# Batch 1's value copies shared by GpSimd and ScalarE, its q loaded ahead of its v, scores and AV moved ahead of transposes, and five unread matmuls fewer

## The chip, the cores and the metric

The kernel runs on one core of one Trainium2 chip. The metric is the time of one execution on the device, in microseconds (us); lower is better. Times vary by about 1% between runs of one kernel (253.42 to 256.43 us in four runs of the kernel before). Every run comes with the TensorE clock that it was granted on average (1.000 is full speed).

Names: PE is TensorE's matmul stream, DVE is VectorE, ACT is ScalarE, POOL is GpSimd. AV is the product of the attention weights and v. In this kernel PSUM holds the results of the matmuls, in tiles that the source calls banks, and SBUF the other tiles. Tiles in the traces: `tkq` and `tv` are the results of `kq_chunk` and `v_chunk` in PSUM, `kqt` and `vt` their copies in SBUF; `qk` are scores, `e_all` exponentials, `av_ps` the AV, `x_ps` transposes; `g_ps`, `v_ps` and `o_ps` are the FFN's gate, value and output products, `th_sb` a tanh, `gs_sb` and `h` what VectorE makes of them.

## The reference, cut to what matters

The first half is block-sorted attention, the second a gated feed-forward block (FFN). Batch 4, 8 heads, 768 rows, head size 64, 8 blocks of 96 rows.

```python
def _attn_ref(q, k, v, sort_net):
    ...                                   # P: sort_net after 5 Sinkhorn rounds
    k_sorted = np.einsum('bhij,bhjcd->bhicd', P, k_b)   # mix the 8 blocks of k
    v_sorted = np.einsum('bhij,bhjcd->bhicd', P, v_b)   # and of v
    scores = scale * np.matmul(q_b, k_sb.transpose(0, 1, 2, 4, 3))
    ...                                   # softmax over each 96x96 block
    return np.matmul(attn, v_sb)

def _moe_ref(x, w_gate, w_val, w_out):
    g = x @ w_gate                        # (3072, 512) @ (512, 1536)
    silu = g * (1.0 / (1.0 + np.exp(-g)))
    val = x @ w_val
    return silu * val @ w_out
```

## The kernel before

The kernel works in bf16 and handles the 3072 tokens as eight FFN blocks of 384 tokens, `ffn(0)` to `ffn(7)`. While TensorE runs one FFN block, the attention work of later tokens is woven into its stream (`merge`): each side task has a place, counted in estimated TensorE microseconds of the FFN block.

Batch 1 needs three things before its attention can start. Its k and q (`kq`) are mixed and transposed by TensorE (`kq_chunk`). Its v is first re-laid in SBUF from (row, feature) to (feature, row) by plain copies into `vch` (`copy_v`), then mixed by TensorE (`v_chunk`). One `v_chunk` reads all rows of `vch`, so it needs every copy.

```python
def copy_v(eng, pair, rows, s, n=4):              # part s of n of the 96 rows
    cs = slice(s * (C // n), (s + 1) * (C // n))
    dst = vch3[rows, :, cs]
    src = v_tiles[pair][rows, cs, :]
    if eng is nc.scalar:
        eng.copy(dst, src.transpose([0, 2, 1]))
    else:
        eng.tensor_copy(dst, src.transpose([0, 2, 1]))
...
for m in range(0, DF, 256):
    load_gv(m, m + 256)                           # the weights, all on one DMA queue
load_k(1, 0, C)
load_v(1, 0, C)
load_q(1, 0, C)
nc.gpsimd.dma_start(out=wo_sb, in_=wo_dram)       # the output weights, last
...
man = tc.manual_schedule(engines={ET.PE, ET.Pool})
man.__enter__()                                   # from here PE and POOL keep program order;
                                                  # the scheduler orders ACT and DVE
...
load_k_pair()
for s in range(4):
    copy_v(nc.gpsimd, 0, highr, s)                # batch 1's v: all four quarters on GpSimd
...
merge(ffn(0), units(0, range(4, 8), (0.0, 5.6)))
merge(ffn(1), kqs(1, (0.3, 2.6, 4.9)) + vs(v_chunk, 16, (6.2, 7.3, 8.4, 9.5)) + units(1, range(4), (11.0, 15.6)))
for s in range(4):
    copy_v(nc.gpsimd, 1, both, s)
nc.vector.memset(kqt_tile("p")[:, 2 * GI * C:], 0.0)
```

`units(b, ...)` are the scores, exponentials (ACT), AVs and transposes of a batch. `fill(tile, n)` issues n matmuls of zeros that nobody reads; they keep TensorE busy during the start. `gate` and `value` take their PSUM banks from a pool ("gen") of three: a gate bank comes free after a tanh on ACT and a product on DVE.

With `manual_schedule`, the source fixes the order of TensorE and GpSimd only. The order of ScalarE and VectorE is chosen when the kernel is compiled.

The softmax here doesn't subtract the row's maximum and nothing guards it: scores larger than these inputs give would overflow.

Of the kernel before, what the change touches and what calls it, by code (L numbers as in the profile page):

```python
# [17 lines left out]
def kernel(  # L18
# [11 lines left out]
    nc = tc.nc  # L30
# [3 lines left out]
    C = S // NB  # L34
# [6 lines left out]
    NKC = DM // 128  # L41
# [42 lines left out]
    def kq_tile(b):  # L84
        if b not in kq_tiles:
            kq_tiles[b] = natp.tile([128, C, D], BF16, name=f"kq{b}", tag="nat")
        return kq_tiles[b]

    def load_k(b, lo, hi):
        nc.gpsimd.dma_start(out=kq_tile(b)[0:R, lo:hi, :], in_=k_nat[b, :, lo:hi, :])  # L90
# [6 lines left out]
    def load_q(b, lo, hi):  # L97
        nc.gpsimd.dma_start(out=kq_tile(b)[R:2 * R, lo:hi, :], in_=q_nat[b, :, lo:hi, :])

    def load_v(b, lo, hi):  # L100
        if b // 2 not in v_tiles:
            v_tiles[b // 2] = vnp.tile([128, C, D], BF16, name=f"v{b // 2}", tag="vn")
        u = b % 2
        nc.gpsimd.dma_start(out=v_tiles[b // 2][u * R:(u + 1) * R, lo:hi], in_=v_nat[b, :, lo:hi, :])
# [4 lines left out]
    def load_gv(lo, hi):  # L109
        load_w(wg_sb, wg_dram, lo, hi)  # L110
        load_w(wv_sb, wv_dram, lo, hi)

    def copy_v(eng, pair, rows, s, n=4):
# [8 lines that stand above are left out]
    ident = const.tile([128, 128], BF16)  # L122
    lowr, highr = slice(0, R), slice(R, 2 * R)
# [16 lines left out]
    for m in range(0, DF, 256):  # L140
        load_gv(m, m + 256)
    load_k(1, 0, C)
    load_v(1, 0, C)
    load_q(1, 0, C)
    nc.gpsimd.dma_start(out=wo_sb, in_=wo_dram)

    rmix = {b: const.tile([128, 2, 2, H2, NB], BF16, name=f"rmix{b}") for b in (0, 1, "p")}
# [29 lines left out]
    def pair_tile(name, tag):  # L177
        return psum.tile([128, 1024], FP32, name=name, tag=tag)

    def bank_tile(name, tag="gen"):  # L180
        return psum.tile([128, 512], FP32, name=name, tag=tag, bufs=3 if tag == "gen" else 1)
# [29 lines left out]
    def drain(eng, dst, src):  # L211
        if eng == "v":
            nc.vector.tensor_copy(dst, src)  # L213
        else:
            nc.scalar.copy(dst, src)  # L215
# [68 lines left out]
    def exps(b, u, wide, pss):  # L284
        n = ecount[0] % 8
        ecount[0] += 2
        if wide is None:
            for two in range(2):
                nc.scalar.activation(e_all[:, n + two, 0:4 * C], pss[two][0:C, 0:4 * C], AF.Exp, scale=scale)
        else:  # L290
            nc.scalar.activation(e_all[:, n:n + 2, 0:4 * C], wide[0:C, :, 0:4 * C], AF.Exp, scale=scale)  # L291
        es[(b, u)] = [e_all[:, n, :], e_all[:, n + 1, :]]

    def qk(b, u, tag="b"):
        exps(b, u, *scores(b, u, tag))

    def av(b, u, tag="a"):
        half, g = divmod(u, H2)
        vt = vts[b // 2][:, b % 2].rearrange("p (h i) e -> p h i e", h=H)
        av_ps = pair_tile("av_ps", tag).rearrange("p (two n) -> p two n", two=2)  # L300
        o = av_ps[:, :, 0:4 * (D + 1)].rearrange("p two (i e) -> p two i e", e=D + 1)
        for two in range(2):
            e = es[(b, u)][two]
            for i4 in range(4):
                nc.tensor.matmul(o[:, two, i4, :], lhsT=e[:, i4 * C:i4 * C + 128],  # L305
                                 rhs=vt[:, 2 * g + two, half * 4 + i4, :],
                                 start=True, stop=True)
        r_sb = ssp.tile([C, 2, 4, 1], FP32, name="r_sb", tag="r")
        nc.vector.reciprocal(r_sb, o[0:C, :, :, D:D + 1])  # L309
        st = ssp.tile([C, 4, 2, D], BF16, name="st", tag="st")  # L310
        nc.vector.tensor_tensor(st.rearrange("p i two d -> p two i d"), o[0:C, :, :, 0:D],  # L311
                                r_sb.to_broadcast([C, 2, 4, D]), op=ALU.mult)
        sts[(b, u)] = st

    def xt_tile(tag, n):
        bank = psum.tile([128, 1024], BF16, name="x_ps", tag=tag, bufs=3 if tag == "gen" else 1)
        return bank[:, 0:n * 4 * C].rearrange("p (g a b) -> p g a b", g=n, b=C)

    def x_to(dst, b, u):
        st = sts.pop((b, u))  # L320
        for i4 in range(4):
            nc.tensor.transpose(dst[:, i4, :], st[:, i4].rearrange("p a b -> p (a b)"),
                                ident[0:C, 0:C])
# [89 lines left out]
    idle_ps = bank_tile("idle_ps", "x")  # L413

    def fill(tile, n):
        for _ in range(n):
            nc.tensor.matmul(tile, lhsT=warm_sb[:, 0:128], rhs=warm_sb, start=True, stop=True)  # L417
# [37 lines left out]
    fill(idle_ps, 2)  # L455
    v_chunk(0, 0, 8, "v", "gen")
    v_chunk(0, 8, 16, "s", "a")
    fill(idle_ps, 2)
    v_chunk(0, 24, 16, "v", "b")
    fill(idle_ps, 2)  # L460
    v_chunk(0, 40, 8, "s", "gen")
    v_chunk(0, 48, 8, "v", "gen")
    v_chunk(0, 56, 8, "s", "gen")
# [17 lines left out]
    idle_ps = bank_tile("idle_ps")  # L481
# [3 lines left out]
    av(0, 1, "b")  # L485
    fill(idle_ps, 1)
    xts[(0, 0)] = xtp.tile([128, H2, TW], BF16, name="xt0_0", tag="xt")
    x01 = xt_tile("x", 2)
    x_to(x01[:, 0], 0, 0)
    fill(idle_ps, 1)  # L490
    qk(0, 3, "gen")
    av(0, 2, "a")
    x_to(x01[:, 1], 0, 1)
    drain("s", xts[(0, 0)][:, 0:2, :], x01.rearrange("p g a b -> p g (a b)"))
    fill(idle_ps, 2)
# [6 lines left out]
    def early(n, kcs):  # L502
        sb, m, name = ((wg_sb, 0, "g_ps"), (wv_sb, 0, "v_ps"), (wg_sb, 1, "g_ps"))[n]
        if n not in first:
            first[n] = psum.tile([128, TW], FP32, name=name, tag="gen", bufs=3)
        for kc in kcs:
            nc.tensor.matmul(first[n], lhsT=sb[:, kc, ts(m, 128)], rhs=xts[(0, 0)][:, kc, :],
                             start=(kc == 0), stop=(kc == NKC - 1))

    early(0, (0,))  # L510
    early(1, (0,))
    x3 = xt_tile("x", 1)
    x_to(x3[:, 0], 0, 3)
    drain("v", xts[(0, 0)][:, 3:4, :], x3.rearrange("p g a b -> p g (a b)"))
    early(0, (1, 2))
    early(1, (1, 2))
    early(0, (3,))
    early(1, (3,))
    early(2, range(NKC))
    gate_out(0, 0, first[0])  # L520
    value_out(0, 0, first[1])
    gate_out(0, 1, first[2])
# [5 lines left out]
    def units(b, us, ats):  # L528
        us = list(us)
        todo = []  # L530
        for n, at in enumerate(ats):
            u, u2 = us[2 * n:2 * n + 2]
            held = []
            todo.append((at, lambda u=u, u2=u2, held=held: (qk(b, u, "b"), held.append(scores(b, u2, "a")))))
            todo.append((at + 1.3, lambda u2=u2, held=held: exps(b, u2, *held[0])))
            for w, tag, t in ((u, "b", 1.9), (u2, "a", 3.6)):
                if b < 2:
                    todo.append((at + t, lambda w=w, tag=tag: av(b, w, tag)))
                    todo.append((at + t + 3.1, lambda w=w: drain("v", *xtr(b, w))))
                else:  # L540
                    todo.append((at + t, lambda w=w, tag=tag: (av(b, w, tag), x_dma(b, w))))
        return todo

    def kqs(b, ats):
        return [(at, lambda n=n: (kq_chunk(b, n * 32, 16, "v", "b"), kq_chunk(b, n * 32 + 16, 16, "s", "a")))
                for n, at in enumerate(ats)]

    def vs(f, size, ats):
        return [(at, lambda m=m: f(1, m * size, size, "sv"[m % 2], "ba"[m % 2])) for m, at in enumerate(ats)]

    def merge(main, side):
        done, k = 0.0, 0
        side = sorted(side, key=lambda t: t[0])
        for c, f in main:
            f()
            done += c
            while k < len(side) and side[k][0] <= done:
                side[k][1]()
                k += 1
        while k < len(side):  # L560
            side[k][1]()
            k += 1

    def ffn(n):
        todo = []
        for m in range(NFC):
            if n > 0 or m > 1:
                todo.append((0.65, lambda m=m: gate(n, m)))
            if n > 0 or m > 0:
                todo.append((0.65, lambda m=m: value(n, m)))  # L570
            if n > 0 and m % 4 == 3:
                for part in range(3):
                    todo.append((0.87, lambda m=m, part=part: outp(n - 1, m // 4, part)))
        return todo

    load_k_pair()
    for s in range(4):
        copy_v(nc.gpsimd, 0, highr, s)
    load_v(2, 0, C)
    load_v(3, 0, C)  # L580
    q_cast(2)
    q_cast(3)
    both = slice(0, 128)
    merge(ffn(0), units(0, range(4, 8), (0.0, 5.6)))
    merge(ffn(1), kqs(1, (0.3, 2.6, 4.9)) + vs(v_chunk, 16, (6.2, 7.3, 8.4, 9.5)) + units(1, range(4), (11.0, 15.6)))
    for s in range(4):
        copy_v(nc.gpsimd, 1, both, s)
    nc.vector.memset(kqt_tile("p")[:, 2 * GI * C:], 0.0)
# [42 lines left out]
```

## Time and profile before

| | before |
|---|---|
| time, first three runs | 253.42, 253.81, 256.43 us; median 253.81 |
| span of the profiled run | 252.2 us, clock 1.00 |
| TensorE busy | 240.6 us, 95% |

From the profile's page: the line of busy us per engine, with the share of the span and the instruction count, then TensorE's busy tenths and its granted clock in 40 slices of 6.3 us.

```profile
PE 240.6 (95%) x2574; PEld 143.3 (57%) x2574; DVE 159.3 (63%) x342; ACT 110.5 (44%) x187; POOL 51.8 (21%) x46
...
PE   5799999699999999999999999999999999999994
...
PEclk9999999999999999999999999999999999999999
```

TensorE is full from the third slice on, except for one 6 and the last slice. The waits view, with the columns total us, times and longest us, names that dip:

```profile
PE tkq L235 <- DMA kq<-in_q_dram: 2.1, 1, 2.1
```

TensorE waits 2.1 us for q of batch 1, from 46.97 to 49.02 us. The next fence is GpSimd's timeline (start, length, engine, line, operation; in brackets its idle time just before and what ended it). The first three lines are the issues of the loads of v, q and `wo_sb`.

```profile
29.11 0.53 POOL L104 DMA_DIRECT2D v<-in_v_dram  x1 [0.83 <-DMA wv_sb<-in_moe_w_val_dram]
30.70 0.52 POOL L98 DMA_DIRECT2D kq<-in_q_dram  x1 [1.06 <-DMA wg_sb<-in_moe_w_gate_dram]
31.75 1.05 POOL L145 DMA_DIRECT2D wo_sb<-in_moe_w_out_dram  x1 [0.54 <-DMA wv_sb<-in_moe_w_val_dram]
...
44.88 11.22 POOL L120 COPY vch<-v 64x1536 bf16<-64x1536 bf16 x4 [9.90 <-DMA v<-in_v_dram]
```

v has landed when the copies start, at 44.88 us, and q at 48.9. The DMA view gives `wo_sb` 24.2 us from issue to landing, so it lands at 55.95 us.

Two more pieces of before's trace are needed later. The first is ScalarE's timeline around 36 us. ScalarE alternates tanh (`th_sb`) and exponentials (`e_all`) and is idle half of the time (busy 44% of the span).

```profile
35.85 0.49 ACT L364 ACTIVATE th_sb<-g_ps 128x384 bf16<-128x384 f32 x1 [1.17 <-PE g_ps L356]
36.96 1.50 ACT L291 ACTIVATE e_all<-qk 96x768 bf16<-96x768 f32 x2 [0.61 <-PE qk L278]
38.36 0.49 ACT L364 ACTIVATE th_sb<-g_ps 128x384 bf16<-128x384 f32 x1
```

The second is VectorE's timeline from 50 us on.

```profile
49.76 1.23 DVE L213 CAST kqt<-tkq 128x1024 bf16<-128x1024 f32 x1 [1.67 <-PE tkq L235]
50.93 0.07 DVE L588 MEMSET kqtp<- 128x16 uint32 x1
...
64.52 1.22 DVE L213 CAST vt<-tv 96x1024 bf16<-96x1024 f32 x1
```

The second line is the `memset` that ends the code shown above. In the source it stands behind all of `merge(ffn(1), ...)`, and so behind VectorE's cast of a value chunk of batch 1, the third line, which ran at 64.52 us. It ran at 50.93 us. So the compile did move an instruction of an engine without fixed order over 13 us ahead of work on the same engine that stands before it in the source.

### The profile page before, as it was taken

To read this page: it belongs to the slowest core of one execution; us is meant where nothing else is said; L and a number is where in the kernel's file an instruction comes from. 1 tells how busy PE (TensorE), PEld (TensorE's weight loads), DVE (VectorE), ACT (ScalarE), POOL (GpSimd) and SP (SyncE) were. 2 spreads that over 40 slices of the span, in tenths; PEclk is the share of its full clock that TensorE was granted. 3 is DMA by queue.
4 is the path that set the end of the run, shared out by engine and by line. 5 is a ranking of instruction groups with operands and counts; after the bars stand their busy time and mean duration, and the time that the engine had idled before them with its cause. 6 is when DMAs were issued, how large, how long until landed. Compare 5 with 4: busy or idle time off the path is not lost.

```text
span 252.2 us, 6061 instructions
## 1 busy us (share of the span) xinstructions
PE 240.6 (95%) x2574; PEld 143.3 (57%) x2574; DVE 159.3 (63%) x342; ACT 110.5 (44%) x187; POOL 51.8 (21%) x46
## 2 busy tenths in 40 slices
PE   5799999699999999999999999999999999999994
PEld 5275566466555666666656555555555565555543
DVE  6768788675756866758668457545854685456700
ACT  3966644256442543455543433443444243332311
POOL 7847430899079000000000000000000000000000
PEclk9999999999999999999999999999999999999999
DMA  6959999999999176110113122111111111100122
GB/s 104 210 88 163 196 215 219 195 227 216 218 160 146 42 169 128 44 42 3 42 24 83 42 46 54 49 44 33 60 57 42 34 57 57 44 9 32 44 83 84
DMA packets 37866, 23.98 MB, mean 95 GB/s; under 512 B 26064, under 2 KB 34000, under 8 KB 37328
## 3 DMA queue, kind: packets, MB, share of 16 engines
q0 software_dynamic: 21328, 14.16, 38.3%
q1 hardware_dynamic: 16512, 9.45, 13.1%
q8 instruction: 20, 0.33, 0.5%
q14 instruction: 6, 0.05, 0.1%
HBM read 28.32 MB, written 7.86 MB: 143 GB/s over the span
## 4 chain that ended last, share of the span: by engine, by line
PE 74%; DMA 15%; DVE 3%; POOL 3%; issue 2%; ACT 1%; DVEq 0%; POOLq 0%
PE o_ps L391 23%; PE v_ps L374 21%; PE g_ps L356 20%; DMA kq<-in_q_dram 7%; DMA kq<-in_k_dram 4%; DMA wg_sb<-in_moe_w_gate_dram 4%; PE tkq L235 3%; PE av_ps L305 2%; PE qk L278 2%; PE tv L257 1%; DVE gs_sb L366 1%; PE o_ps L407 1%; DVE vt L213 1%; POOL wg_sb L107 1%; POOL wv_sb L107 1%
## 5 line engine op out<-in xcount | busy, mean ns | idle before, releaser
L366 DVE SCALAR_TENSOR_TENSOR gs_sb<-th_sb,g_ps 128x384 bf16<-128x384 bf16 x96 | 52.7, 549 | 52.9 <-ACT th_sb L364 50.7
L374 PE MATMUL v_ps<-xt,wv_sb 128*128 128x384 bf16 x380 | 77.3, 326 | 0.3
L356 PE MATMUL g_ps<-xt,wg_sb 128*128 128x384 bf16 x376 | 76.5, 325 | 0.0
L364 ACT ACTIVATE th_sb<-g_ps 128x384 bf16<-128x384 f32 x96 | 47.2, 491 | 57.7 <-PE g_ps L356 54.9
L391 PE MATMUL o_ps<-wo_sb,h 128*128 128x512 bf16 x276 | 64.5, 379 | 0.0
L379 DVE SCALAR_TENSOR_TENSOR h<-v_ps,gs_sb 128x384 bf16<-128x384 f32 x96 | 53.3, 555 | 6.9 <-DVE gs_sb L366 0.5
L374 PEld LDWEIGHTS <-wv_sb 128*128 128x128 bf16 x380 | 35.4, 97 | 23.6 <-issue 1.5
L356 PEld LDWEIGHTS <-wg_sb 128*128 128x128 bf16 x376 | 34.6, 97 | 22.9
L391 PEld LDWEIGHTS <-h 128*128 128x128 bf16 x276 | 26.1, 98 | 27.7
L396 ACT COPY o_sb<-o_ps 128x512 f32<-128x512 f32 x23 | 13.5, 586 | 51.4 <-PE o_ps L391 51.4
L120 POOL COPY vch<-v 64x1536 bf16<-64x1536 bf16 (+1 forms) x10 | 28.0, 2839 | 18.7 <-DMA v<-in_v_dram 18.7
L291 ACT ACTIVATE e_all<-qk 96x768 bf16<-96x768 f32 x30 | 22.5, 802 | 6.2 <-PE qk L278 6.2
L311 DVE TENSOR_TENSOR st<-av_ps,r_sb 96x512 bf16<-96x512 f32 x32 | 21.7, 680 | 0.2
L305 PEld LDWEIGHTS <-e_all 96*128 96x128 bf16 x256 | 12.3, 98 | 5.1 <-ACT e_all L291 0.9
L305 PE MATMUL av_ps<-vt,e_all 96*128 96x65 bf16 x256 | 13.5, 194 | 0.2 <-ACT e_all L291 0.2
L213 DVE CAST vt<-tv 96x1024 bf16<-96x1024 f32 (+1 forms) x9 | 9.8, 1100 | 4.3 <-PE tv L247 4.3
L215 ACT CAST vt<-tv 96x1024 bf16<-96x1024 f32 (+1 forms) x9 | 9.1, 1030 | 5.6 <-PE tv L247 2.9
L309 DVE RECIPROCAL r_sb<-av_ps 96x8 f32<-96x8 f32 x32 | 6.4, 199 | 6.1 <-PE av_ps L305 6.1
L235 PE MATMUL tkq<-rmix,kq 128*64 128x64 bf16 x384 | 7.4, 197 | 2.1 <-DMA kq<-in_q_dram 2.1
L417 PE MATMUL idle_ps<-warm_sb 128*128 128x512 bf16 x30 | 9.2, 396 | 0.0
L215 ACT CAST kqt<-tkq 128x1024 bf16<-128x1024 f32 (+1 forms) x7 | 6.0, 894 | 7.0 <-PE tkq L235 7.0
L213 DVE CAST kqt<-tkq 128x1024 bf16<-128x1024 f32 (+1 forms) x7 | 7.5, 1069 | 2.6 <-PE tkq L235 2.4
(79 smaller groups left out, 135.4 us busy)
## 6 DMA issues: line engine op xcount, KB each, us to landing
out_dram<-o_sb SPq DMA_DIRECT2D x23, 256.0 KB, 2.0
v<-in_v_dram POOLq DMA_DIRECT2D x3, 768.0 KB, 14.1
kq<-in_q_dram POOLq DMA_DIRECT2D x2, 768.0 KB, 13.8
wg_sb<-in_moe_w_gate_dram POOLq DMA_DIRECT2D x6, 256.0 KB, 9.0
wv_sb<-in_moe_w_val_dram POOLq DMA_DIRECT2D x6, 256.0 KB, 9.4
wo_sb<-in_moe_w_out_dram POOLq DMA_DIRECT2D x1, 1536.0 KB, 24.2
kp<-in_k_dram POOLq DMA_DIRECT2D x2, 768.0 KB, 27.3
q_scr<-in_q_dram POOLq DMA_DIRECT2D x2, 768.0 KB, 20.6
```

The source lines that it names most:

```text
L120: eng.tensor_copy(dst, src.transpose([0, 2, 1]))
L213: nc.vector.tensor_copy(dst, src)
L215: nc.scalar.copy(dst, src)
L291: nc.scalar.activation(e_all[:, n:n + 2, 0:4 * C], wide[0:C, :, 0:4 * C], AF.Exp, scale=scale)
L305: nc.tensor.matmul(o[:, two, i4, :], lhsT=e[:, i4 * C:i4 * C + 128], rhs=vt[:, 2 * g + two, half * 4 + i4, :], start=True, stop=True)
L311: nc.vector.tensor_tensor(st.rearrange("p i two d -> p two i d"), o[0:C, :, :, 0:D], r_sb.to_broadcast([C, 2, 4, D]), op=ALU.mult)
L356: nc.tensor.matmul(g_ps, lhsT=wg_sb[:, kc, ts(m, 128)], rhs=xt[:, kc, :], start=(kc == 0), stop=(kc == NKC - 1))
L364: nc.scalar.activation(th_sb, g_ps, AF.Tanh, scale=0.5)
L366: nc.vector.scalar_tensor_tensor(gs_sb, th_sb, 1.0, g_ps, op0=ALU.add, op1=ALU.mult)
L374: nc.tensor.matmul(v_ps, lhsT=wv_sb[:, kc, ts(m, 128)], rhs=xt[:, kc, :], start=(kc == 0), stop=(kc == NKC - 1))
L379: nc.vector.scalar_tensor_tensor(h_tiles[n][:, m, :], v_ps, 0.5, gs_tiles.pop(m), op0=ALU.mult, op1=ALU.mult)
L391: nc.tensor.matmul(o_ps, lhsT=h_w[:, m, ts(t3, 128)], rhs=wo_sb[:, m, :], start=(m == 0), stop=(m == NFC - 1))
```

## The change

The intent: take five unread matmuls out of the start; let the scores of unit 3 and AV 2 run before the transposes so that the first FFN block starts earlier; load q of batch 1 ahead of v, because q is what TensorE waits for; and, since v then comes later, shorten its copies by giving the last quarter to ScalarE in four pieces.

```diff
     load_k(1, 0, C)
+    load_q(1, 0, C)
     load_v(1, 0, C)
-    load_q(1, 0, C)
...
     v_chunk(0, 8, 16, "s", "a")
-    fill(idle_ps, 2)
     v_chunk(0, 24, 16, "v", "b")
-    fill(idle_ps, 2)
...
+    qk(0, 3, "gen")
+    av(0, 2, "a")
     x01 = xt_tile("x", 2)
     x_to(x01[:, 0], 0, 0)
-    fill(idle_ps, 1)
-    qk(0, 3, "gen")
-    av(0, 2, "a")
     x_to(x01[:, 1], 0, 1)
... (the first matmuls of the first FFN block regrouped, none added or removed)
-    for s in range(4):
+    for s in range(3):
         copy_v(nc.gpsimd, 0, highr, s)
...
-    merge(ffn(0), units(0, range(4, 8), (0.0, 5.6)))
-    merge(ffn(1), kqs(1, (0.3, 2.6, 4.9)) + vs(...) + units(1, ...))
+    kq1 = kqs(1, (11.9, 0.8, 3.4))
+    merge(ffn(0), units(0, range(4, 8), (0.0, 5.6)) + kq1[:1])
+    merge(ffn(1), [(0.6 + 1.3 * n, lambda n=n: copy_v(nc.scalar, 0, highr, 12 + n, 16)) for n in range(4)]
+          + kq1[1:] + vs(...) + units(1, ...))
```

More of the change, by code (lines that the diff above doesn't have):

```diff
@@ L508, in early @@
                              start=(kc == 0), stop=(kc == NKC - 1))
-    early(0, (0,))
-    early(1, (0,))
+    early(0, (0, 1))
+    early(1, (0, 1))
     x3 = xt_tile("x", 1)
@@ L514 @@
     drain("v", xts[(0, 0)][:, 3:4, :], x3.rearrange("p g a b -> p g (a b)"))
-    early(0, (1, 2))
-    early(1, (1, 2))
+    early(0, (2,))
+    early(1, (2,))
+    early(2, (0,))
     early(0, (3,))
     early(1, (3,))
-    early(2, range(NKC))
+    early(2, (1, 2, 3))
     gate_out(0, 0, first[0])
@@ L583 @@
     both = slice(0, 128)
-    merge(ffn(0), units(0, range(4, 8), (0.0, 5.6)))
-    merge(ffn(1), kqs(1, (0.3, 2.6, 4.9)) + vs(v_chunk, 16, (6.2, 7.3, 8.4, 9.5)) + units(1, range(4), (11.0, 15.6)))
+    kq1 = kqs(1, (11.9, 0.8, 3.4))
+    merge(ffn(0), units(0, range(4, 8), (0.0, 5.6)) + kq1[:1])
+    merge(ffn(1), [(0.6 + 1.3 * n, lambda n=n: copy_v(nc.scalar, 0, highr, 12 + n, 16)) for n in range(4)]
+          + kq1[1:] + vs(v_chunk, 16, (6.2, 7.3, 8.4, 9.5)) + units(1, range(4), (11.0, 15.6)))
     for s in range(4):
```

## The prediction

> **What bounds the kernel now.** The page: PE busy 240.6 of 252.2 us (95%), clock 1.00 throughout. From 29 us to the end PE is a dense stream. The waits view shows one large PE wait after the start: `tkq` <- DMA `kq<-in_q_dram`, 2.1 us, at 46.97 to 49.02. The chain of waits is DMA before 49 us (k, weights, q of batch 1), then nearly all PE. So only the stretch from 12.7 to about 60 us can give anything.
>
> **What the change does, costed.**
> 1. Five unread 128x512 matmuls go, 0.213 us each back to back (five took 1.25 us, the last 0.40): 1.07 us of PE in a stretch where the drains wait for PE (gaps of 0.4 to 1.1 us before casts). About 0.8 us back before the first scores (now 21.4 us).
> 2. Scores of unit 3 and AV 2 ahead of the transposes: unit 3's exponential can start at 24.0 (score banks free) instead of 24.94; this shortens a PE-ACT-DVE chain, about 0.4 to 0.6 us. The dense stream (28.98 us now) starts about 1.4 us earlier.
> 3. q of batch 1 is loaded before v. The queue is first in, first out (packets view), 768 KB every 4.1 us: v lands now at 44.8, q at 48.9; they swap. The first kq chunk moves to about 43.3 us (new time), so PE waits some 1.4 us for q instead of 2.05.
> 4. v then lands at about 48.9. GpSimd's three copies take 3 x 2.81 = 8.4 us, done at 57.5 (now 56.1). ACT's four pieces: from 1.51 us for 64x768 I estimate 0.8 us each, 3.3 us where ACT is half idle.
>
> **The new limit.** `wo_sb` is last in that queue: issued at 31.75, 24.2 us to landing, so 55.95 us, unchanged by the swap. The first `o_ps` matmul runs now at 57.37. My sum brings PE there at about 55.2, so it waits some 0.8 us. Of a nominal 2 us only 57.37 - 56.05 = 1.3 survives. The value chunks, 1.75 us later (57.8), find `vch` ready at 57.5, 0.3 us to spare. After that PE is back to back with the same work, so 1.3 us is the end-to-end gain.
>
> **Prediction:** 253.8 - 1.3 = 252.5 us; 8 in 10: 251.3 to 253.7. Faster by over 2%: 2%; within 2%: 96%; slower by over 2%: 2%.
>
> **What would show it.** Dense stream about 1.4 us earlier; the wait for `kq<-in_q_dram` ends near 44.8 and is 1 to 1.6 us; a new PE wait of 0.5 to 1.2 us at the first `o_ps`, released by the `wo_sb` DMA at about 56 us; GpSimd's copies end near 57.5; first `o_ps` to the end keeps its length; span about 250.9.
>
> **What would make it wrong.** ACT's order is left to the scheduler: a copy put ahead of a tanh before v has landed blocks ACT, PE runs out of PSUM buffers, up to 2 us lost. If GpSimd is slower, the value chunks wait. If `wo_sb` lands earlier, the gain reaches 2 us. The removed matmuls might let the clock drop: [...] here the 2.05 us idle showed no drop, and the new gaps are shorter.

The clause that is cut from it is about the clock. It is no term of the sum, which stays as it was: 253.8 - 1.3 = 252.5 us.

## The result, and the profile after

The changed kernel took 267.31 us (median of 4 runs, 266.33 to 267.82), before 254.92 us (median of 4 runs, 253.42 to 256.43). The ratio is 1.048, with a 95% interval of 1.040 to 1.057: slower by almost 5%. Ratios here are the mean time of one kernel's runs over that of the other's of the same rounds, so they are not quite the ratio of the medians. The granted clock was 0.968 to 0.974 in all four runs.

The page of the changed kernel, the same lines as above; a slice is now 6.6 us:

```profile
PE 240.2 (90%) x2544; PEld 143.9 (54%) x2569; DVE 159.7 (60%) x342; ACT 113.6 (43%) x191; POOL 48.9 (18%) x45
...
PE   5698970199999999999999999999999999999994
...
PEclk9999995569999999999999999999999999999999
```

Busy times have hardly changed (TensorE 240.2 against 240.6 us; of its matmuls the trace lacks some 25, the 2569 weight loads show the five fewer), but TensorE has two slices that are almost empty (0 and 1), and in three slices its clock is 0.5 to 0.6. The waits view of TensorE and then that of ScalarE:

```profile
PE av_ps L305 <- ACT e_all L291: 12.7, 2, 12.5
```

```profile
ACT vch L118 <- DMA v<-in_v_dram: 13.7, 1, 13.7
```

TensorE waits 12.5 us at one place for one exponential. ScalarE waits 13.7 us at one place for v. ScalarE's timeline shows how the two belong together:

```profile
34.85 0.49 ACT L364 ACTIVATE th_sb<-g_ps 128x384 bf16<-128x384 f32 x1 [1.17 <-PE g_ps L356]
49.08 0.84 ACT L118 COPY vch<-v 64x384 bf16<-64x384 bf16 x1 [13.74 <-DMA v<-in_v_dram]
49.95 1.50 ACT L291 ACTIVATE e_all<-qk 96x768 bf16<-96x768 f32 x2
```

Before, the tanh at 35.85 us was followed by the exponential `e_all` at 36.96. Now the next instruction in ScalarE's queue is a copy of v, and v lands only at 49 us. The copy itself takes 0.84 us, but it stands at the head of the queue for 13.7 us, and the exponential, whose scores are ready, stands behind it. TensorE's timeline:

```profile
37.50 0.82 PE L356 MATMUL g_ps<-xt,wg_sb 128*128 128x384 bf16 x4
50.81 0.62 PE L305 MATMUL av_ps<-vt,e_all 96*128 96x65 bf16 x8 [12.49 <-ACT e_all L291]
52.47 1.44 PE L374 MATMUL v_ps<-xt,wv_sb 128*128 128x384 bf16 x4 [1.04 <-DVE gs_sb L366]
...
70.62 1.89 PE L391 MATMUL o_ps<-wo_sb,h 128*128 128x512 bf16 x7
```

TensorE goes on for 3 us after ScalarE has stopped (to 38.3 us); then the AV needs that exponential. GpSimd's timeline and a table by stretch (busy us and count of PE, weight loads, DVE, ACT, POOL, then the clock, DMA share and GB/s) complete the picture:

```profile
30.16 0.52 POOL L104 DMA_DIRECT2D v<-in_v_dram  x1 [0.77 <-DMA wg_sb<-in_moe_w_gate_dram]
...
49.11 8.30 POOL L120 COPY vch<-v 64x1536 bf16<-64x1536 bf16 x3 [14.39 <-DMA v<-in_v_dram]
```

```profile
38.30:50.80 12.50, 0.02 (x1) 0.00 (x0) 0.00 (x0) 1.69 (x3) 1.69 (x1) 0.60 1.07 206
50.80:57.20 6.40, 5.35 (x30) 2.97 (x31) 3.64 (x9) 4.50 (x7) 6.40 (x3) 0.50 1.20 225
```

The loads are as predicted: v lands at 49.1 us and GpSimd's three copies end at 57.4 (49.11 + 8.30). In the wait of 12.5 us nothing but the DMA works until v lands at 49 us, and after it the clock is 0.50 for over 6 us.

On ScalarE nothing passed the copy in 13.7 us: the exponential behind it, whose scores TensorE had finished by 36.1 us, ran at 49.95 us.

### The profile page after: what moved, and what is told of

The parts are those of the page before. It is cut to its first block, busy times and chain, and to the rows that moved or that the text cites. A ratio compares the mean times of both kernels' runs of the same rounds, so it can differ in the third digit from the quotient of the medians.

```text
span 265.5 us, 6029 instructions
## 1 busy us (share of the span) xinstructions
PE 240.2 (90%) x2544; PEld 143.9 (54%) x2569; DVE 159.7 (60%) x342; ACT 113.6 (43%) x191; POOL 48.9 (18%) x45
## 4 chain that ended last, share of the span: by engine, by line
PE 74%; DMA 15%; DVE 3%; POOL 3%; issue 2%; ACT 1%; DVEq 0%; ACTq 0%; POOLq 0%
PE v_ps L374 22%; PE o_ps L391 22%; PE g_ps L356 20%; DMA v<-in_v_dram 7%; DMA kq<-in_k_dram 4%; DMA wg_sb<-in_moe_w_gate_dram 3%; PE tkq L235 3%; PE av_ps L305 2%; PE qk L278 2%; PE tv L257 1%; DVE gs_sb L366 1%; PE o_ps L407 1%; DVE vt L213 1%; POOL wg_sb L107 1%; POOL wv_sb L107 1%
## 5 line engine op out<-in xcount | busy, mean ns | idle before, releaser
L374 PE MATMUL v_ps<-xt,wv_sb 128*128 128x384 bf16 x380 | 78.7, 330 | 1.3 <-DVE gs_sb L366 1.0
L356 PE MATMUL g_ps<-xt,wg_sb 128*128 128x384 bf16 x376 | 77.8, 330 | 0.0
L391 PE MATMUL o_ps<-wo_sb,h 128*128 128x512 bf16 x256 | 62.2, 379 | 1.1
L120 POOL COPY vch<-v 64x1536 bf16<-64x1536 bf16 (+1 forms) x9 | 25.1, 2822 | 27.9 <-DMA v<-in_v_dram 15.0
L305 PE MATMUL av_ps<-vt,e_all 96*128 96x65 bf16 x256 | 14.1, 197 | 12.8 <-ACT e_all L291 12.7
L305 PEld LDWEIGHTS <-e_all 96*128 96x128 bf16 x256 | 12.5, 100 | 18.4 <-ACT e_all L291 13.7
L118 ACT COPY vch<-v 64x768 bf16<-64x768 bf16 (+1 forms) x8 | 9.3, 1186 | 13.8 <-DMA v<-in_v_dram 13.7
```

Source lines behind the costliest of these rows:

```text
L305: nc.tensor.matmul(o[:, two, i4, :], lhsT=e[:, i4 * C:i4 * C + 128], rhs=vt[:, 2 * g + two, half * 4 + i4, :], start=True, stop=True)
L356: nc.tensor.matmul(g_ps, lhsT=wg_sb[:, kc, ts(m, 128)], rhs=xt[:, kc, :], start=(kc == 0), stop=(kc == NKC - 1))
L374: nc.tensor.matmul(v_ps, lhsT=wv_sb[:, kc, ts(m, 128)], rhs=xt[:, kc, :], start=(kc == 0), stop=(kc == NKC - 1))
L391: nc.tensor.matmul(o_ps, lhsT=h_w[:, m, ts(t3, 128)], rhs=wo_sb[:, m, :], start=(m == 0), stop=(m == NFC - 1))
```

## The experiments

The theory to test (A): the compile put ScalarE's copies too early into its queue, ScalarE stood until v landed, and everything else follows. Rivals: (B) the swap of q and v or the early kq chunk stalls TensorE; (C) the removed unread matmuls let the clock fall; (D) ScalarE simply got too much work. Eleven runs were made, on three chips, each beside runs of the kernel before on the same chip. All were correct.

| run | median us | ratio to before | 95% interval | clock of its runs |
|---|---|---|---|---|
| changed kernel, again | 267.56 | 1.051 | 1.046 to 1.056 | 0.968 to 0.974 |
| act_in_order | 253.41 | 0.997 | 0.992 to 1.001 | 0.992 to 1.000 |
| four_on_gpsimd | 255.75 | 1.006 | 1.001 to 1.010 | 0.993 to 1.000 |
| kept_busy | 267.32 | 1.052 | 1.049 to 1.056 | 0.998 to 1.000 |
| pe_part_alone | 255.23 | 1.004 | 1.000 to 1.008 | 0.993 |
| one_copy_early | 260.33 | 1.024 | 1.020 to 1.028 | 0.980 to 0.987 |
| v_before_q | 267.26 | 1.051 | 1.047 to 1.055 | 0.974 |
| no_wait_left | 252.25 | 0.992 | 0.989 to 0.995 | 0.998 to 1.000 |
| nwl_free | 268.82 | 1.057 | 1.051 to 1.063 | 0.966 to 0.972 |
| before_act_order | 254.81 | 1.001 | 0.995 to 1.007 | 0.993 to 1.000 |
| no_wait_left_2 | 251.22 | 0.988 | 0.983 to 0.992 | 0.993 to 1.000 |

### 1. ScalarE in program order

```diff
-    man = tc.manual_schedule(engines={ET.PE, ET.Pool})
+    man = tc.manual_schedule(engines={ET.PE, ET.Pool, ET.Activation})
... (and back to PE and POOL alone behind merge(ffn(1), ...))
```

> The changed kernel with ScalarE's instructions of the first two FFN blocks kept in program order, so that no copy of v can be moved ahead of the exponential of unit 6. Theory A (the copies were put into ScalarE's queue at 35 us, v landed at 49 us, and the queue stood still): the 12.5 us PE wait on e_all is gone, ScalarE waits for v under 1.5 us, the granted clock is 1.00 throughout, time 251.5 to 253.5 us, some 14 us under the changed kernel. Rival B (q ahead of v, or the early place of the first kq chunk, is what stalls PE): still above 262 us. Rival C (the removed unread matmuls let the clock fall): the clock still falls near 40 us and the time stays above 260 us.

It took 253.41 us, 14 us less than the changed kernel (by medians, on another chip). The 12.5 us wait is gone. ScalarE's timeline, then the largest wait in TensorE's stream after the start, then the stretch behind it:

```profile
50.52 0.49 ACT L364 ACTIVATE th_sb<-g_ps 128x384 bf16<-128x384 f32 x1 [1.86 <-PE g_ps L356]
51.04 0.88 ACT L118 COPY vch<-v 64x384 bf16<-64x384 bf16 x1
```

```profile
PE tkq L235 <- DMA kq<-in_q_dram: 2.2, 1, 2.2
```

```profile
45.00:50.00 5.00, 4.62 (x79) 2.94 (x80) 2.62 (x5) 1.50 (x2) 1.19 (x1) 0.67 1.09 194
```

The first copy now runs at 51.04 us, right behind the tanh, and waits for nothing, because v landed 2 us earlier. One edit to the order took the whole loss away, while q ahead of v, the early kq chunk and the five missing matmuls all stayed. That rejects B. It did not meet the expectation in one point: in this profiled run the clock did fall, to 0.67 in the stretch from 45 to 50 us, behind a TensorE wait of 2.24 us for q. Of the four runs, two had a clock of 0.992 (254.11 and 253.85 us) and two 1.000 (252.98 and 252.11 us).

A control asks whether the fixed order is worth something by itself:

> A control: the kernel before with ScalarE in program order in the first two FFN blocks and nothing else. If the fixed order is worth something by itself, this is faster than before; I expect the same within 0.5 us, 253.5 to 254.5.

The kernel before with the same edit took 254.81 us, ratio 1.001 (0.995 to 1.007): the same, though the median lies 0.3 us above the expected range. So the fixed order only undoes the harm.

### 2. All four copies on GpSimd

```diff
-    for s in range(3):
+    for s in range(4):
         copy_v(nc.gpsimd, 0, highr, s)
...
-    merge(ffn(1), [(0.6 + 1.3 * n, lambda n=n: copy_v(nc.scalar, 0, highr, 12 + n, 16)) for n in range(4)]
-          + kq1[1:] + vs(...) + units(1, ...))
+    merge(ffn(1), kq1[1:] + vs(...) + units(1, ...))
```

> The changed kernel without ScalarE's four pieces: GpSimd copies all four quarters of batch 1's v. Theory A: no wait of 12 us; v lands at 49, GpSimd ends at about 60.3 us, so the first value chunk (reached at about 57.8) waits some 2.5 us; 253.5 to 255.5 us, clock 1.00. Rivals B and C: still above 260 us.

It took 255.75 us, just above the expected range, and in the profiled run the clock was 0.993 instead of the expected 1.00. TensorE's waits:

```profile
PE tv L247 <- POOL vch L120: 2.3, 1, 2.3
...
PE o_ps L391 <- DVE gs_sb L366: 0.6, 1, 0.6
```

With nothing of v on ScalarE the big wait is gone as well, so A holds a second time. The value chunk waits 2.3 us for GpSimd's last copy, as worked out. The second line is a wait of 0.6 us ahead of the first `o_ps`, which ran at 55.39 us. The profile puts it down to a VectorE product, which frees a bank. The tanh before it ended at 54.81 us, and such a product takes 0.55 us (mean of before), so by estimate it ended at about 55.4. `wo_sb`, issued at 31.62 us, landed 23.7 us later, at 55.3. Both end within 0.1 us of the start of `o_ps`, so the run does not separate them: that this is the wait for `wo_sb` that the prediction had forecast is possible, not shown.

### 3. TensorE kept busy through the wait

```diff
     merge(ffn(0), units(0, range(4, 8), (0.0, 5.6)) + kq1[:1]
+          + [(7.45, lambda: fill(bank_tile("busy_ps", "x"), 57))])
```

> The changed kernel with 57 unread 128x512 matmuls (12.2 us) in PE's stream just ahead of the AV that waits 12.5 us: same wait for ScalarE, but PE is busy through it. If the low clock after the wait (0.50 from 42 to 57 us) comes from PE's idleness, the clock stays at 1.00, the AV still starts near 50.8 us, and the time falls by 2 to 3.5 us, to about 264.5. If the clock fell for another reason, the time stays at 267.

The clock part of the expectation came true, the time part did not: the clock was 0.998 to 1.000 in all runs, but the time was 267.32 us, as the changed kernel's 267.31 and 267.56. TensorE's timeline:

```profile
38.12 12.47 PE L417 MATMUL busy_ps<-warm_sb 128*128 128x512 bf16 x55
50.76 0.43 PE L305 MATMUL av_ps<-vt,e_all 96*128 96x65 bf16 x8 [0.17 <-ACT e_all L291]
52.42 0.81 PE L374 MATMUL v_ps<-xt,wv_sb 128*128 128x384 bf16 x4 [1.24 <-DVE gs_sb L366]
...
54.61 0.81 PE L374 MATMUL v_ps<-xt,wv_sb 128*128 128x384 bf16 x4 [0.73 <-DVE gs_sb L366]
...
69.93 1.89 PE L391 MATMUL o_ps<-wo_sb,h 128*128 128x512 bf16 x7
```

The unread matmuls fill the wait (the trace has 55 of the 57) and the AV starts at 50.76 us as before. But after it TensorE waits 1.24 and then 0.73 us for products that hang on ScalarE's tanh. ScalarE has a backlog from standing: two exponentials, three more copies and the tanh, until 55.4 us. In the changed kernel the slow clock hides behind that same backlog. The first `o_ps` comes at 69.93 instead of 70.62 us: in the profile the low clock costs at most 0.7 us, and the times do not show even that. So nearly all of the loss is ScalarE's standing: the wait and the backlog behind it. The run also shows that the low clock came from TensorE's idleness: the same wait, filled, left the clock at 0.998 to 1.000, where the changed kernel had 0.968 to 0.974.

### 4. The TensorE part of the change alone

The kernel before with the five unread matmuls out and the scores, AV and first matmuls rearranged; the loads, the copies and the kq chunks stay as before.

> The kernel before with the first part of the change alone (five fewer unread matmuls, scores of unit 3 and AV 2 ahead of the transposes, the early matmuls regrouped); loads, copies and kq chunks as before. Theory A: the dense stream starts about 1 us earlier, PE then waits for q of batch 1 about 3 us instead of 2.05 (it lands at 48.9 as before), and the time is that of before within 0.5 us; clock 1.00. Rival C: slower than before, clock below 1.00 after 13 us.

It took 255.23 us, ratio 1.004 (1.000 to 1.008), all four runs at a clock of 0.993. Both parts of the expectation were missed: by medians it is 1.3 us slower than before, not within 0.5, and the clock was not 1.00. Its wait for q, and its stretches:

```profile
PE tkq L235 <- DMA kq<-in_q_dram: 2.6, 1, 2.6
```

```profile
45.00:50.00 5.00, 2.42 (x70) 1.87 (x68) 2.31 (x4) 0.68 (x2) 4.96 (x2) 0.90 1.09 193
50.00:55.00 5.00, 5.00 (x87) 3.00 (x82) 2.81 (x6) 1.99 (x3) 5.00 (x3) 0.76 1.29 225
```

In the changed kernel, where the same edit is in, the first full `v_ps` group starts at 27.98 instead of 28.98 us, so it does what it was meant to, 1 us instead of the predicted 1.4. Alone it gains nothing, since TensorE then stands in front of the same q: the wait grows to 2.58 us, and behind it the clock was low: means of 0.90 and 0.76 in two stretches of 5 us are 3.4 us at a clock of 0.50 (1.0 and 2.4). That is an estimate. It takes this clock to be at either 1.00 or 0.50, as in the trace of the changed kernel, where it is 1.00 until 40.7 us, 0.50 from 40.8 to 57.7 and 1.00 from 57.8 on; in pe_part_alone the stretches before 45 us and from 55 us on have 1.00. The runs fit C in kind: with this edit all four had a clock of 0.993, where the seven runs of before on the same chip had 1.000. They do not fit it in the size: in act_in_order the two runs with the lower clock took 1.4 us more than the two at 1.000 (253.98 against 252.55, means), and the loss to explain is 13.

### 5. The place of one copy in the queue

act_in_order with its first copy moved ahead by hand, to where ScalarE comes at about 40 us:

```diff
     merge(ffn(0), units(0, range(4, 8), (0.0, 5.6)) + kq1[:1]
+          + [(9.2, lambda: copy_v(nc.scalar, 0, highr, 12, 16))])
...  (and for n in range(1, 4) in ffn(1))
```

> The kernel act_in_order with one change: ScalarE's first piece (64x384) is put by hand two tanh ahead of the kq drain, so that it reaches the head of ScalarE's queue at about 40 us, 9 us before v lands. Theory A (a queue in order stands behind one copy whose data has not come): ScalarE idle about 9 us until 49, PE waits on DVE or ScalarE from about 43 to about 51 us, time 258 to 261 us. Rival (the loss came from the amount of work put on ScalarE, not from where one copy stands): as act_in_order, 253.4.

It took 260.33 us, within the expected range; the interval of the ratio, 1.020 to 1.028, begins just at the 2% line, so the verdict is "unclear", but it lies well above 1. ScalarE's timeline and TensorE's largest wait:

```profile
39.21 0.49 ACT L364 ACTIVATE th_sb<-g_ps 128x384 bf16<-128x384 f32 x1 [1.07 <-PE g_ps L356]
48.92 0.84 ACT L118 COPY vch<-v 64x384 bf16<-64x384 bf16 x1 [9.22 <-DMA v<-in_v_dram]
```

```profile
PE v_ps L374 <- DVE gs_sb L366: 8.7, 1, 8.7
```

One copy of 0.84 us, at the wrong place in an ordered queue, costs 7 us against act_in_order (260.33 - 253.41, on another chip). The amount of work on ScalarE is the same in both, which rejects D. ScalarE stands 9.2 us and TensorE 8.7 us. TensorE's way into the wait is another than in the changed kernel: `v_ps` waits for the bank that a tanh and a product free, and not for an exponential.

### 6. Only the order of the loads undone

The changed kernel with v loaded ahead of q again.

> The changed kernel with only the order of the loads undone (v ahead of q, v lands at about 44.9). The compiled order shows ScalarE's first copy moved up by three tanh, to about 31 us. Theory A: ScalarE stands again some 13 us, now from 31 to 45, PE waits 11 to 13 us, 264 to 268 us. Rival B (the swap of q and v is the cause): about 254. Rival B2 (the copy's place is fixed and only the landing counts): about 263.

It took 267.26 us, although v now lands at 44.4 us. ScalarE's timeline:

```profile
30.26 0.49 ACT L364 ACTIVATE th_sb<-g_ps 128x384 bf16<-128x384 f32 x1
44.43 1.60 ACT L118 COPY vch<-v 64x384 bf16<-64x384 bf16 x2 [13.69 <-DMA v<-in_v_dram]
```

TensorE's largest wait is 14.1 us, where 11 to 13 were expected:

```profile
PE v_ps L374 <- DVE gs_sb L366: 14.1, 1, 14.1
```

The copies moved ahead too: they now stand behind the tanh of 30.26 us instead of that of 34.85, and ScalarE stands 13.7 us again. B would have given 254 us, a fixed place 263 us. In the source the copies had not moved at all. What had moved is one load in the queue. This fits a compile that places the copies by its own estimate of when v lands, and which put them some 14 us too early in both kernels (49.08 against 35.34, 44.43 against 30.75). That this is how the scheduler decides is inferred from the orders it produced; nothing here looks inside it.

### 7. A version without waits, and the same with ScalarE's order free

The limits that the traces gave are q landed by 45.4, v by 49, `vch` complete at about 57.5 and `wo_sb` at 56 us. So no_wait_left takes act_in_order, puts the kq chunks back to their places of before (TensorE is there at 45.9 us), the copies to 3.0 and later, and the first output matmuls, the value chunks and the units of batch 1 behind 56 us:

```diff
-    kq1 = kqs(1, (11.9, 0.8, 3.4))
+    kq1 = kqs(1, (0.3, 2.6, 4.9))
...
-    merge(ffn(1), [(0.6 + 1.3 * n, lambda n=n: copy_v(nc.scalar, 0, highr, 12 + n, 16)) for n in range(4)]
-          + kq1[1:] + vs(v_chunk, 16, (6.2, 7.3, 8.4, 9.5)) + units(1, range(4), (11.0, 15.6)))
+    merge(ffn(1), [(3.0 + 1.3 * n, lambda n=n: copy_v(nc.scalar, 0, highr, 12 + n, 16)) for n in range(4)]
+          + kq1 + vs(v_chunk, 16, (8.6, 9.5, 10.4, 11.3)) + units(1, range(4), (12.0, 16.6)))
... (no kq chunk in ffn(0) any more; in ffn(1) the three output tiles follow m = 5, 8, 11 instead of 3, 7, 11)
```

> A version meant to beat both: the first part of the change, q of batch 1 ahead of v, three quarters of v on GpSimd and four pieces on ScalarE, but ScalarE in program order in the first two FFN blocks, its pieces from 3.0 on (PE then at about 50 us, v landed at 49), the kq chunks back at their places of before (PE there at 45.9 us, q landed at 44 to 45.4), and the first output matmuls two column blocks later (PE there at about 57, wo_sb landed at 56). Theory A: no PE wait over 0.7 us between 25 and 60 us, clock 1.00, 250 to 251.5 us, ratio to before about 0.989. If the limits that I read (q, v, wo landing) are wrong, a wait for one of them stays.

It took 252.25 us, ratio 0.992 (0.989 to 0.995), a little above the expected 251.5; the gain of 0.8% is clear of noise. No wait for q, v or `wo_sb` is left; what is left is one wait for a bank of the last value chunk:

```profile
PE qk L278 <- DVE vt L213: 1.2, 1, 1.2
```

nwl_free is the same source with the one line back that leaves ScalarE's order to the compile. TensorE, GpSimd and the loads have the same instructions in the same order.

> The kernel no_wait_left with one line back: ScalarE's order is left to the scheduler again. TensorE, GpSimd and the loads have the same instructions in the same order; in the compiled order ScalarE's first copy stands again before the exponential of unit 6, although the source has it 2.4 FFN-us later than the changed kernel did. Theory A: ScalarE stands about 13.7 us until v lands at 49, PE waits 12 us, 265 to 268 us. If anything else than ScalarE's order made the difference, it stays near 252.

It took 268.82 us, 16.6 us more than no_wait_left (by medians, on another chip). ScalarE's timeline and TensorE's largest wait:

```profile
34.83 0.49 ACT L364 ACTIVATE th_sb<-g_ps 128x384 bf16<-128x384 f32 x1 [1.17 <-PE g_ps L356]
48.73 0.84 ACT L118 COPY vch<-v 64x384 bf16<-64x384 bf16 x1 [13.41 <-DMA v<-in_v_dram]
```

```profile
PE av_ps L305 <- ACT e_all L291: 12.4, 2, 12.2
```

This is the sharpest test. In the source the copies stand 2.4 us of TensorE work later than in the changed kernel; in the queue they stand at the same place, behind the tanh of 34.83 us. Nothing but ScalarE's and VectorE's order differs from a kernel that is faster than before.

no_wait_left_2 moves the units of batch 1 to 13.3 and 17.2:

> no_wait_left with the scores of batch 1 some 1.3 us later in the PE stream, so that they no longer wait 1.2 us for the last value chunk's bank. If that wait is the last one left, 251.0 to 251.6 us; if the later units collide with the next FFN block, as no_wait_left, 252.25.

It took 251.22 us, ratio 0.988 (0.983 to 0.992): 1.2% faster than before. The largest wait left after the start is 0.5 us, for GpSimd's last copy:

```profile
PE tv L247 <- POOL vch L120: 0.5, 1, 0.5
```

## Why the prediction was wrong

**What bounds the kernel before: right.** TensorE is full, q of batch 1 is the one large wait, and pe_part_alone shows that starting earlier gains nothing while q lands late.

**Unread matmuls and reordering: right in kind, 1.0 us instead of 1.4.** The first full `v_ps` group moved from 28.98 to 27.98 us.

**The swap of q and v: right in kind.** The loads landed in the order of their issue: before, v, q and `wo_sb`, issued at 29.11, 30.70 and 31.75 us, landed at 44.9, 48.9 and 55.95; in the changed kernel q, issued at 28.86, landed at 45.2 and v, issued at 30.16, at 49.1 (48.9 forecast for v). In act_in_order q had landed by 45.4 us (44.8 forecast); the wait for it was 2.24 us, where the prediction said 1 to 1.6. In four_on_gpsimd q landed at 43.9 us (issued at 28.64, 15.3 us to landing) and nothing waited for it: its landing moves by more than a microsecond between runs.

**The copies: right as durations.** ScalarE's pieces took 0.84 us (0.8 forecast), GpSimd ended at 57.4 us (57.5 forecast).

**The wait for `wo_sb`: possible, not shown.** four_on_gpsimd has 0.6 us at that place, where a product on VectorE ends at the same time.

**The step that failed** is the one in the prediction's last paragraph: "ACT's order is left to the scheduler: a copy put ahead of a tanh before v has landed blocks ACT, PE runs out of PSUM buffers, up to 2 us lost." The mechanism was named, but given a small chance and too small a size. The prediction does not say where it took the copies to stand, but a loss of up to 2 us fits only a place shortly before v's landing. In act_in_order, which keeps the source's order, the first one ran at 51.04 us, after the landing; left to the compile it stood at the head of the queue from 35.3 us on. ScalarE stood 13.7 us, TensorE stopped 3 us later and waited 12.5 us. The path was in part another too: in the changed kernel TensorE waited for an exponential, not for a PSUM buffer behind a tanh; the path that the prediction named is the one seen in v_before_q (14.1 us) and one_copy_early (8.7 us). The estimate "ACT is half idle" was true and beside the point: what the copy cost ScalarE was its wait plus its duration, and the wait was 16 times the duration (13.74 over 0.84).

That this term is the whole loss is shown by act_in_order: with it gone, the two runs at full clock took 252.98 and 252.11 us, on either side of the forecast 252.5; the median of all four was 253.41, inside the range. The forecast gain of 1.3 us is not shown by it: against the runs of before on the same chip the ratio is 0.997, and its interval (0.992 to 1.001) holds both that gain and none.

**The clock: named, and misjudged.** The prediction said that the new gaps would be shorter than 2.05 us and leave the clock alone. TensorE waits of 2.24 us (act_in_order), 2.58 us (pe_part_alone), 2.43 us (before_act_order) and 2.27 us (four_on_gpsimd) were followed by a low clock in the profiled run; 2.05 us in the profiled run of before was not. Of three of these kernels (all but pe_part_alone) other runs kept a clock of 1.000, with waits that were not traced. So one run without a drop behind 2.05 us said little about waits a few tenths of a microsecond longer. By estimate the low spell, taken to be at 0.50, lasted 3.4 us in all four: that is what the means of their stretches of 5 us below 1.00 come to (0.67 and 0.99; 0.90 and 0.76; 0.95 and 0.71; 0.66). On the two later chips 5 of 22 runs of the kernel before had a clock of 0.993, and they took 254.69 to 256.55 us, against 253.18 to 254.59 for the others. In the changed kernel the clock fell to 0.50 within the 12.5 us wait, at 40.8 us, and stayed there until 57.8 us, but that cost at most 0.7 us in time.

## What to carry to other kernels

When work is put on an engine whose order the compiler chooses, ask where in that engine's queue it will land, not only whether the engine has time: an instruction whose data comes from a DMA can stop everything behind it (here one copy of 0.84 us held ScalarE for 13.7 us). If the DMA's landing matters, fix the order of that engine by hand around it, and check in the trace that the engine's idle time in front of the instruction is short. A trace of the kernel before can already show how far the compiler moves instructions: look for one that ran long before work of the same engine that stands ahead of it in the source.
